# Rows of three blocks moved within SBUF in place of a store and a reload, in a Fourier mixing layer with an MLP

## The chip, the cores and the metric

One core of a Trainium2 chip runs the whole kernel. The metric is device time in microseconds. One execution is profiled as well; its trace gives the start and duration of every instruction on PE (TensorE), DVE (VectorE), ACT (ScalarE), POOL (GpSimd) and SP (SyncE, which here only issues DMAs), and of the DMA traffic.

## The reference

For one sequence of 2048 rows of 640 columns (fp32), a layer norm is followed by two branches that are summed with the input:

```python
xn = _layernorm(x, axis=-1)
return x + _A_ref(xn, seq_re, seq_im, hid_re, hid_im) + _B_ref(xn, w1, b1, w2, b2)

# A: real part of a DFT along the hidden and then the sequence dimension
a = jnp.einsum("bsd,ed->bse", x, dft_hid_re)
b = jnp.einsum("bsd,ed->bse", x, dft_hid_im)
y = jnp.einsum("ts,bse->bte", dft_seq_re, a) - jnp.einsum("ts,bse->bte", dft_seq_im, b)

# B: an MLP of 640 -> 1536 -> 640
h = _gelu(jnp.einsum("bsd,df->bsf", x, w1) + b1)
return jnp.einsum("bsf,fd->bsd", h, w2) + b2
```

The four DFT matrices are inputs: 640 x 640 (called wr and wi in the kernel) and 2048 x 2048 (cr and ci).

## The kernel before, in words

**Arithmetic.** PE multiplies in a rounded fp32 form. Each operand is split into a high half, which ACT makes (`high`), and a low half, which DVE makes as the difference (`low`); a product is then three matmuls, high by high, high by low and low by high (`product`, lines 308 to 310; in `hidden`, line 326). Many products are formed by schemes with fewer multiplications and more sums, and the sums of the operands ("forms") are made on DVE ahead of the matmuls.

**Blocks.** The rows are worked in four blocks of 512 (block 0 to 3), each as four tiles of 128 rows (`xt[c]`, c from 0 to 15). The MLP of block 0 comes first. A loop over i from 0 to 9 (the steps of `background(i)`) does for each of twelve groups of 128 MLP columns the hidden product `hidden(i + 2)` (15 matmuls), the GELU and split of the result (tile hs), and `output(i)` (15 matmuls on W2), so a step is 30 matmuls. W1 and W2 are loaded by SP, split by `prep_w1` and `prep_w2` and kept in places (`PLACES`: xab0 to xab3, xc01, xc23, as, r01, rt2), which later hold other things. In between, `background(i)` prepares blocks 1 and 2, which are called "a" and "b".

**Rows.** A block's tiles are loaded by SP (`load_x`), DVE takes the statistics (`ln_stats`, two instructions of 320 columns and a small one for each tile), `ln_scale` makes the reciprocal deviations, and `ln_apply` normalises in place. Then `put_rows` stores the tiles from POOL's queue to a DRAM tensor xs, and `load_z` loads them again from there in another arrangement, z: partition q * 32 + r of z holds quarter q of the columns of the rows r, 32 + r, 64 + r and so on. From z, DVE's 32 x 32 transposes (`transpose_z`) give what PE needs with the columns on partitions. xs is read once more, much later: `by_chunks` copies it to xn, from which the Fourier part takes its rows. Block 0 goes another way: PE transposes its normalised tiles into five PSUM banks (`transpose_x`), and ACT and DVE split these into XT. One of its tiles (`last`) is normalised on ACT, the others on DVE.

**Pairs.** `pair(k)`, k from 0 to 5, does the hidden products of blocks 1 and 2 together on two groups of columns, with seven windows of matmuls; it has six points (`beside_pair(k, at)`, in the order 2, 5, 6, 3, 7, 4) at which other work is put on the engines: the sums of block 0 (`finish(0, ...)`: a bias on ACT, a turn on DVE, an add into xo on POOL), their store to ys (`store_sums`), and the forms of wr and wi (`load_w`, `turn_w`, and `prep_w(j, n)` with n from 0 to 2 for each fifth j; they lie in the tile wst and are stored to DRAM as wits). zc is a copy of a window's result that ACT makes behind the GELU of the pair's first group.

**Between.** After the pairs, a loop over p does the output products of block 2 from units kept in DRAM (`load_unit`), and `between(p)` does beside it the sums of block 1 (xo(1), loaded by `load_xo(1, ...)` into the place xab2), the rows of block 3, the turns of these at p of 7 to 9, and the weights for block 3. `OBANKS` gives the PSUM banks of each block's five output groups; the fourth and fifth group of block 2 use the banks that the fourth and fifth of block 1 leave.

**The rest** is the hidden product of block 3 and the Fourier part: eight stages of sequence products and two of hidden products (`hidden_beside`), whose results are turned, added and stored (`store`).

**Order.** The program writes out the order of each engine's instructions by hand, and every engine runs its own in that order. An instruction that waits therefore holds all that stand behind it on its engine, and so do a DMA's waits on the queue that issues it (SP, POOL or ACT). Tiles with a tag share a place with `bufs` copies; a new tile waits until the last reader of the old one is done, a DMA that reads it included.

Of the kernel before, what the change touches and what calls it, by code (L numbers as in the profile page):

```python
# [20 lines left out]
NGATE = 4  # L21
# [5 lines left out]
def kernel(  # L27
# [134 lines left out]

    row_places = rows.tile([P, NC, D], F32, name="row")
# [5 lines left out]
    def chunked(ap):  # L169

        return ap.rearrange("p (c q i) -> p q c i", q=Q, i=B)
# [63 lines left out]
    def ln_apply_chunked(dst, c):  # L235

        m = MV[:, slot[c]]
        nc.vector.tensor_scalar(
            chunked(dst),
            xt[c].rearrange("p (q c i) -> p q c i", q=Q, i=B),  # L240
            m[:, 0:1],
            m[:, 3:4],
            op0=ALU.subtract,
            op1=ALU.mult,
        )
# [70 lines left out]
    def hidden(g):  # L316
        i = g % NF
        acc = bank((5 if g < NF else 0) + g % 3)
        kinds = ((0, 0), (0, 1), (1, 0))
        steps = [(j, k) for j in range(ND) for k in range(3)]  # L320
        if g == 0:

            steps.sort(key=lambda s: s[1] == 1)
        for n, (j, k) in enumerate(steps):
            a, b = kinds[k]
            nc.tensor.matmul(  # L326
                acc, W1[i][:, a, j * P : (j + 1) * P], XT[j][:, b], start=n == 0, stop=n == len(steps) - 1
            )
        return acc
# [321 lines left out]
    for c in (1, 0, 2, 3):  # L651
        load_x(c)
# [19 lines left out]
    for q in range(Q):  # L672
        nc.sync.dma_start(b2c[q * B : (q + 1) * B], b2[q * DQ : (q + 1) * DQ].rearrange("(c i) -> i c", i=B))

    for p in PLACES:
        open_place(*p)
# [5 lines left out]
    def transpose_x(c):  # L682
        for j in range(ND):
            nc.tensor.transpose(tacc[j][:, c * P : (c + 1) * P], xp[:, c, j * P : (j + 1) * P], ident)
# [19 lines left out]
    nc.scalar.activation(xp[:, last], xp[:, last], AF.Copy, scale=MV[:, last, 3:4])  # L704
# [8 lines left out]
    load_w1(4)  # L713
    acc0 = hidden(0)
# [7 lines left out]

    def background(i):

        if i == 0:
            for c in range(NC):
                ln_apply(c, put=False)
            A["rows_b"] = zo_tile("rows_b", (P, NC, D))
            for c in range(2 * NC, 3 * NC):
                load_x(c, home=A["rows_b"])  # L730
            for c in range(NC):
                put_rows(c)
        if i == 1:
            ln_stats(8)
            ln_stats(9)
            for c in range(NC, 2 * NC):
                load_x(c)
        if i == 2:
            ln_stats(10)
            ln_stats(11)  # L740
            ln_scale(NC)
            for c in range(2 * NC, 3 * NC):
                ln_apply(c)
            Z["b"] = zo_tile("z_b")
            load_z(Z["b"], 2)
        if i == 3:
            for c in range(NC, 2 * NC):
                ln_stats(c)
        if i == 4:
            ln_scale(NC)  # L750
            for c in range(NC, 2 * NC):
                ln_apply(c)
            Z["a"] = as_z(row_places)
            load_z(Z["a"], 1)
        if i == 5:
            new_forms(0, "vb", "ua", "va")
            make_forms("b", "vb0", "vb1", "ob0")
        if i == 6:
            new_forms(3, "t1")
            make_forms("a", "ua0", "ua1", "oa0")  # L760
        if i == 7:
            make_forms("a", "va0", "va1")
        if i >= 7:
            (ua, va), (ub, vb) = ((Z[k][:, :, : 2 * B], Z[k][:, :, 2 * B : 4 * B]) for k in "ab")
        if i == 7:
            add(ub, ub, ua, ALU.subtract)
        if i == 8:
            make_forms("b", "t10", "t11")
            add(vb, vb, ub, ALU.subtract)
        if i == 9:  # L770
# [102 lines left out]
    def finish(t, *es, home=None):  # L873

        for e in es:
            add_block(xo[t], e, oacc[t][e], f"ot{t}_{e}", bias=b2c[:, e : e + 1], **(home or {}))
# [5 lines left out]
    def store_sums(t):  # L882
        for k, (c0, c1) in enumerate(YCOLS):
            nc.gpsimd.dma_start(ys[k][t], xo[t][:, :, c0:c1])
# [5 lines left out]
    def beside_pair(k, at):  # L890

        if k == 0:
            if at == 5:
                make_forms("a", "t30", "t31")
            if at == 6:
                make_forms("a", "t40", "t41")
                load_w(0, 0)
                load_w(1, 0)
            if at == 4:
                finish(0, 0, 1)  # L900
            return
        j = k - 1
        if k == 1:
            if at == 2:
                finish(0, 2, home=in_zt)
            if at == 5:
                finish(0, 3, home=in_zt)
                finish(0, 4)
            if at == 6:
                store_sums(0)  # L910
# [6 lines left out]
        steps = {7: (0,), 4: (1,)} if k == 1 else {3: (0,), 7: (1, 2) if k == LASTK else (1,), 4: () if k == LASTK else (2,)}  # L917
        if k == 2 and at == 5:
            prep_w(0, 2)
# [7 lines left out]
        if k == 1 and at == 7:  # L927
            A["wst"] = zo_tile("wst", (P, NB * DQ), F32R)
# [69 lines left out]
    def between(p):  # L998
# [4 lines left out]
        if p == 1:  # L1003
            finish(1, 3, 4, home=in_zt)
            ln_stats(14)
        if p == 2:
            ln_stats(15)
            ln_scale(NC)
            for c in range(3 * NC, 4 * NC):
                ln_apply(c)  # L1010
# [391 lines left out]
    def hidden_beside(b, n):  # L1402
# [68 lines left out]
        v1 = lambda: add(s(1, "v1"), s(1, "v1"), x_)  # L1471
        pre = [v1] if n == 17 and not last else []
# [4 lines left out]
            3: [to(ya[:, :, : 2 * B], x_, f"ya1_{ta}")],  # L1477
            4: [t2(0)],
# [12 lines left out]
            17: [v1, yb2, yb2] if last else [yb1, yb2],  # L1491
# [144 lines left out]
```

## Time and profile before

| | |
|---|---|
| runs | 883.66, 880.26, 881.50 us; median 881.5 |
| the profiled execution | 883.43 us, of which the traced span is 881.6 |
| mean granted clock of TensorE | 0.988 |
| matmuls | 3711, of which 19 warm the clock up and 20 transpose block 0 |
| bytes | 124.92 MB read from and 51.38 MB written to HBM |

In the rows of a timeline stand the start in us, the time that the instruction (or a merged group of xN) covers, the engine, the line, the operation, the tiles (out<-in), and in brackets the idle time of the engine just before and what ended it. `POOLq`, `SPq` and `ACTq` are the queues that issue DMAs. A matmul's duration of 0.39 us is that of one in a pipeline; the distance of two starts says what it costs. Instructions of different kinds overlap a little on DVE and ACT as well.

### The profile page before, as it was taken

What the parts mean: (1) busy time and instruction counts of PE and PEld (TensorE: products, weight loads), DVE (VectorE), ACT (ScalarE), POOL (GpSimd) and SP (SyncE); (2) the same over time, 40 slices, a digit from 0 to 9 for tenths busy, and PEclk for the clock granted to TensorE, in tenths of its full rate; (3) what the DMA queues carried; (4) which work ended last, traced back from release to release, by engine and by line L of the source; (5) the groups of instructions that cost most, each with busy time, mean ns of one, the idle gap of its engine ahead of it and who ended that gap; (6) DMA issues with size and microseconds to landing.
All of it is one profiled execution on the core that took longest, in us unless ns stands there. A gap on an engine that the chain in (4) does not pass through costs nothing.

```text
span 881.6 us, 10526 instructions
## 1 busy us (share of the span) xinstructions
PE 853.3 (97%) x3711; PEld 700.4 (79%) x3711; DVE 682.6 (77%) x888; ACT 366.7 (42%) x527; POOL 79.2 (9%) x111
## 2 busy tenths in 40 slices
PE   7998998999969999999999999999999999999997
PEld 6886776888748888888888888888888888888885
DVE  6786975875734477998989888888977988886586
ACT  6554564655414456543443434332232432323241
POOL 0230043333240500000000000000000000000000
PEclk9999999999978999999999999999999999999999
DMA  7985559988988695987774259946475679904364
GB/s 195 297 264 122 112 143 280 308 236 285 256 244 202 155 355 229 168 167 173 185 161 149 59 145 324 247 96 179 115 186 183 223 214 217 337 19 173 120 166 102
DMA packets 200035, 171.76 MB, mean 195 GB/s; under 512 B 65232, under 2 KB 171216, under 8 KB 199344
## 3 DMA queue, kind: packets, MB, share of 16 engines
q1 hardware_dynamic: 187168, 142.13, 60.5%
q0 software_dynamic: 7536, 28.06, 9.3%
q10 hardware_dynamic: 5280, 0.92, 0.5%
q8 instruction: 29, 0.48, 0.2%
q14 instruction: 22, 0.18, 0.1%
HBM read 124.92 MB, written 51.38 MB: 200 GB/s over the span
## 4 chain that ended last, share of the span: by engine, by line
PE 80%; DMA 8%; DVE 5%; SPq 2%; issue 2%; POOL 1%; ACT 1%; DVEq 0%; ACTq 0%; POOLq 0%
PE banks L309 25%; PE banks L310 25%; PE banks L308 25%; PE banks L326 5%; DMA w1r<-in_B_w_dram 3%; DMA xs<-row 2%; DMA row<-in_A_x_dram 1%; DVE xab L186 1%; SPq L286 1%; SPq L399 1%; DMA row<-xs 1%; DMA rows_b<-in_A_x_dram 1%; PE banks L666 1%; DVE st L212 1%; DVE w1f L186 0%
## 5 line engine op out<-in xcount | busy, mean ns | idle before, releaser
L308 PE MATMUL banks<-as,xab 128*128 128x512 f32 x407 | 158.3, 389 | 0.0
L310 PE MATMUL banks<-as,xab 128*128 128x512 f32 x407 | 158.3, 389 | 0.0
L309 PE MATMUL banks<-as,xab 128*128 128x512 f32 x407 | 158.3, 389 | 0.0
L183 ACT ACTIVATE as<-r 128x1024 fp32r<-128x1024 f32 x80 | 85.0, 1062 | 173.6 <-PE banks L310 148.7
L186 DVE TENSOR_TENSOR as<-r,as 128x1024 fp32r<-128x1024 f32 x80 | 97.2, 1216 | 38.8 <-ACT as L183 38.8
L309 PEld LDWEIGHTS banks<-as,xab 128*128 128x128 f32 x407 | 76.4, 188 | 16.0
L308 PEld LDWEIGHTS banks<-as,xab 128*128 128x128 f32 x407 | 76.4, 188 | 15.9
L310 PEld LDWEIGHTS banks<-as,xab 128*128 128x128 f32 x407 | 76.4, 188 | 15.8
L308 PE MATMUL banks<-as,xc 128*128 128x512 f32 x224 | 87.1, 389 | 0.0
L309 PE MATMUL banks<-as,xc 128*128 128x512 f32 x224 | 87.1, 389 | 0.0
L310 PE MATMUL banks<-as,xc 128*128 128x512 f32 x224 | 87.1, 389 | 0.0
L183 ACT ACTIVATE as<-rt 128x1024 fp32r<-128x1024 f32 x32 | 34.0, 1062 | 69.8 <-PE banks L310 57.9
L326 PE MATMUL banks<-xt,xab 128*128 128x512 f32 x240 | 56.8, 390 | 0.2 <-ACT xt L183 0.2
L186 DVE TENSOR_TENSOR hs<-ab,hs 128x512 fp32r<-128x512 f32 x36 | 26.3, 732 | 34.2 <-ACT hs L183 33.9
L326 PEld LDWEIGHTS banks<-xt,xab 128*128 128x128 f32 x240 | 44.7, 188 | 10.2 <-ACT xt L183 1.3
L309 PEld LDWEIGHTS banks<-as,xc 128*128 128x128 f32 x224 | 42.0, 188 | 8.8
L310 PEld LDWEIGHTS banks<-as,xc 128*128 128x128 f32 x224 | 42.0, 188 | 8.7
L308 PEld LDWEIGHTS banks<-as,xc 128*128 128x128 f32 x224 | 42.0, 188 | 8.7
L308 PE MATMUL banks<-hs,xc 128*128 128x512 f32 x120 | 46.9, 391 | 1.3 <-DVE ot L385 1.3
L309 PE MATMUL banks<-hs,xc 128*128 128x512 f32 x120 | 46.8, 390 | 0.2 <-DVE hs L186 0.2
L310 PE MATMUL banks<-hs,xc 128*128 128x512 f32 x120 | 46.7, 390 | 0.0
L186 DVE TENSOR_TENSOR as<-rt,as 128x1024 fp32r<-128x1024 f32 x32 | 38.8, 1212 | 5.3 <-ACT as L183 5.3
(213 smaller groups left out, 1661.4 us busy)
## 6 DMA issues: line engine op xcount, KB each, us to landing
raw<-in_A_dft_seq_re_dram SPq DMA_DIRECT2D x64, 256.0 KB, 5.6
raw<-in_A_dft_seq_im_dram SPq DMA_DIRECT2D x64, 256.0 KB, 5.2
w1r<-in_B_w_dram SPq DMA_DIRECT2D x144, 80.0 KB, 3.4
wit<-wst POOLq DMA_DIRECT2D x15, 384.0 KB, 4.0
ws<-wit SPq DMA_DIRECT2D x15, 384.0 KB, 5.5
xn<-xs SPq DMA_DIRECT2D x4, 1280.0 KB, 7.0
wit<-wst POOLq DMA_DIRECT2D x20, 256.0 KB, 4.4
forms_ab<-xab SPq DMA_DIRECT2D x4, 1280.0 KB, 7.3
```

The lines of the kernel that those rows point to most:

```text
L183: nc.scalar.activation(h, s, AF.Copy)
L186: nc.vector.tensor_tensor(l, s, h.bitcast(F32), op=ALU.subtract)
L212: nc.vector.bn_stats(st[:, h, :], xt[c][:, h * half : (h + 1) * half])
L286: eng.dma_start(t[q * B : (q + 1) * B], v[q, :, :, f0 : f0 + P])
L308: nc.tensor.matmul(acc, wh, mh, start=first, stop=False, skip_group_check=goes_on)
L309: nc.tensor.matmul(acc, wh, ml, start=False, stop=False, skip_group_check=goes_on)
L310: nc.tensor.matmul(acc, wl, mh, start=False, stop=last, skip_group_check=goes_on)
L326: nc.tensor.matmul(acc, W1[i][:, a, j * P : (j + 1) * P], XT[j][:, b], start=n == 0, stop=n == len(steps) - 1)
L399: nc.sync.dma_start(t[q * B : (q + 1) * B], v[:, :, s0 : s0 + B])
L666: nc.tensor.matmul(wacc, warm[:, :P], warm, start=True, stop=True)
```

## The change

**Rows in SBUF.** `put_z(z, rows)` makes z straight from the normalised tiles: 16 DMAs from POOL's queue, each from 32 partitions to 32 others, with runs of 160 numbers. It takes the place of `load_z` for blocks 1, 2 and 3. `put_rows` follows it for all tiles of the block, so xs is written as before. The tiles of block 2 are loaded right after XT's split into the place r01, and those of block 1 in step 0 into the place rt2 (`rows_in`); both belong to later parts of W2, so these two places are opened for W2 in steps 4 and 7, and not at the start. The statistics, forms and sums of blocks 1 and 2 move to earlier steps; step 9 has none of them left.

**Start.** The tiles of block 0 are loaded in the order 0 to 3. They are normalised and transposed in two parts, columns 0 to 255 and 256 to 639. W1 of the first group is split by hand: its high half on ACT between the two parts, its low half on DVE behind both. `hidden(0)` and `hidden(1)` use new orders of their matmuls. `NGATE` changes which of three warm-up tiles each of the 19 warm-up matmuls reads: 7, 3 and 9 in place of 4, 4 and 11; the loads of w1 go into the same buffers. The loads of b2 come later.

**Sums and forms.** The sums of block 0 are stored as soon as each part is complete. The forms of the first fifth of wr and wi (j of 0) move from points 7, 4 of pair 1 and 5 of pair 2 to point 4 of pair 1 and points 2 and 5 of pair 2. The sums of block 1 are added on DVE in place of POOL.

**End.** The last 32 columns of each quarter of a block's result are turned the other way and added into the PSUM bank in `hidden_beside`, so that the final turn writes the result and no add follows.

```diff
-NGATE = 4
+NGATE = (7, 10)
+    def rows_in(tag):
+        return place(tag, (P, 4096), F32)[:, : NC * D].rearrange("p (k d) -> p k d", k=NC)
 # hidden(g)
-            steps.sort(key=lambda s: s[1] == 1)
+            steps = FIRST
+        if g == 1:
+            steps.sort(key=lambda s: s[1] == 2)
+    FIRST = [(0, 0), (1, 0), (0, 2), (1, 2), (2, 0), (2, 2), (0, 1), (3, 0), (3, 2)]
+    FIRST += [(1, 1), (4, 0), (4, 2), (2, 1), (3, 1), (4, 1)]
-    for c in (1, 0, 2, 3):
+    for c in range(NC):
         load_x(c)
-        warm = warms[min(k // NGATE, 2)]
+        warm = warms[sum(k >= n for n in NGATE)]
-    for p in PLACES:
+    for p in PLACES[:7]:
         open_place(*p)
-    nc.scalar.activation(xp[:, last], xp[:, last], AF.Copy, scale=MV[:, last, 3:4])
-    for c in (0, 2, last, 3):
-        if c != last:
-            ln_apply_chunked(xp[:, c], c)
-        transpose_x(c)
-    prep_w1(0)
+    W1[0], first_w1 = slots[1, 0], w1r.pop(0).rearrange("p a b -> p (a b)")
+    for j0, j1 in ((0, 2), (2, ND)):
+        part = xp[:, last, j0 * P : j1 * P]
+        nc.scalar.activation(part, part, AF.Copy, scale=MV[:, last, 3:4])
+        if j0 == 0:
+            nc.scalar.activation(W1[0][:, 0], first_w1, AF.Copy)
+        for c in (0, last, 2, 3):
+            if c != last:
+                ln_apply_chunked(xp[:, c], c, j0, j1)
+            transpose_x(c, j0, j1)
+    nc.vector.tensor_tensor(W1[0][:, 1], first_w1, W1[0][:, 0].bitcast(F32), op=ALU.subtract)
     for j in range(ND):
         split(XT[j][:, 0], XT[j][:, 1], tacc[j])
+    A["rows_b"] = rows_in("r01")
+    for c in range(2 * NC, 3 * NC):
+        load_x(c, home=A["rows_b"])
     load_w1(3)
     load_w1(4)
+    # the four loads of b2c, which stood before open_place
+    def put_z(z, rows):
+        for a in range(NC):
+            for q in range(Q):
+                nc.gpsimd.dma_start(
+                    z[q * B : (q + 1) * B].rearrange("r (c a) d -> r a c d", a=NC)[:, a],
+                    rows[a * B : (a + 1) * B, :, q * DQ : (q + 1) * DQ],
+                )
 # background(i), as it is after the change
+        if i == 0:
+            for c in range(NC):
+                ln_apply(c)
+            A["rows_a"] = rows_in("rt2")
+            for c in range(NC, 2 * NC):
+                load_x(c, home=A["rows_a"])
+            for c in range(2 * NC, 3 * NC):
+                ln_stats(c)
+        if i == 1:
+            ln_scale(NC)
+            Z["b"] = zo_tile("z_b")
+            for c in range(2 * NC, 3 * NC):
+                ln_apply(c, put=False)
+            put_z(Z["b"], A["rows_b"])
+            for c in range(2 * NC, 3 * NC):
+                put_rows(c)
+            ln_stats(NC)
+            ln_stats(NC + 1)
+        if i == 2:
+            ln_stats(NC + 2)
+            ln_stats(NC + 3)
+            ln_scale(NC)
+            Z["a"] = as_z(row_places)
+            for c in range(NC, 2 * NC):
+                ln_apply(c, put=False)
+            put_z(Z["a"], A["rows_a"])
+            for c in range(NC, 2 * NC):
+                put_rows(c)
+        if i == 4:
+            open_place(*PLACES[7])
+            new_forms(0, "vb", "ua", "va")
+            make_forms("b", "vb0", "vb1", "ob0")
+        if i == 5:
+            make_forms("a", "ua0", "ua1", "va0")
+        if i == 6:
+            new_forms(3, "t1")
+            make_forms("a", "oa0", "va1")
+            add(ub, ub, ua, ALU.subtract)
+        if i == 7:
+            open_place(*PLACES[8])
+            make_forms("b", "t10", "t11")
+            add(vb, vb, ub, ALU.subtract)
+        if i == 8:
+            turn_x("t20", "b")
+            turn_x("t21", "b")
+            add(ua, vb, ua, ALU.subtract)
+            add(va, va, vb, ALU.subtract)
+            load_xo(0)
 # beside_pair(k, at)
-            if at == 6:
-                store_sums(0)
+            # store_sums(0, 0) at point 4 of pair 0, (0, 1) and (0, 2) behind finish(0, 3) and finish(0, 4)
-        steps = {7: (0,), 4: (1,)} if k == 1 else {...}
-        if k == 2 and at == 5:
-            prep_w(0, 2)
+        steps = {4: (0,)} if k == 1 else {...}
+        if k == 2 and at in (2, 5):
+            prep_w(0, 1 if at == 2 else 2)
 # between(p)
-            finish(1, 3, 4, home=in_zt)
+            finish(1, 3, 4, home=in_zt, eng=nc.vector)
+            Z["z"] = zo_tile("z3")
             for c in range(3 * NC, 4 * NC):
-                ln_apply(c)
-            Z["z"] = zo_tile("z3")
-            load_z(Z["z"], 3)
+                ln_apply(c, put=False)
+            put_z(Z["z"], row_places)
+            for c in range(3 * NC, 4 * NC):
+                put_rows(c)
-            finish(1, p - 4)
+            finish(1, p - 4, eng=nc.vector)
 # hidden_beside and the end
+        def last_columns():
+            A["end"] = A["rt2"][:, 0, 0, 0]
+            nc.vector.transpose(A["end"].rearrange("p (n i) -> p n i", i=B), ya[:, :, 3 * B : 4 * B])
+        end = lambda: add(bank(X + 1), bank(X + 1), A["end"])
+            2: [last_columns] if last else [],
-            17: [v1, yb2, yb2] if last else [yb1, yb2],
+            17: [v1, end, yb2, yb2] if last else [yb1, yb2],
-        add_turned(d, turned(bank(X + k - 2), f"yt_{k}"))
+        if k == 3:
+            nc.vector.transpose(d, bank(X + 1).rearrange("p (n i) -> p n i", i=B))
+        else:
+            add_turned(d, turned(bank(X), f"yt_{k}"))
```

More of the change, by code (lines that the diff above doesn't have):

```diff
@@ L671 @@
     load_w2(2)
-    for q in range(Q):
-        nc.sync.dma_start(b2c[q * B : (q + 1) * B], b2[q * DQ : (q + 1) * DQ].rearrange("(c i) -> i c", i=B))
-    for p in PLACES:
+    for p in PLACES[:7]:
         open_place(*p)
@@ L680, with transpose_x @@
     xp = zo_tile("xp", (P, NC, D))
-    def transpose_x(c):
-        for j in range(ND):
+    def transpose_x(c, j0, j1):
+        for j in range(j0, j1):
             nc.tensor.transpose(tacc[j][:, c * P : (c + 1) * P], xp[:, c, j * P : (j + 1) * P], ident)
@@ L720 @@
     load_w1(5)
+    def put_z(z, rows):
+        for a in range(NC):
+            for q in range(Q):
+                nc.gpsimd.dma_start(
+                    z[q * B : (q + 1) * B].rearrange("r (c a) d -> r a c d", a=NC)[:, a],
+                    rows[a * B : (a + 1) * B, :, q * DQ : (q + 1) * DQ],
+                )
     def background(i):
@@ L729, in background @@
             for c in range(2 * NC, 3 * NC):
-                load_x(c, home=A["rows_b"])
-            for c in range(NC):
                 put_rows(c)
-        if i == 1:
-            ln_stats(8)
-            ln_stats(9)
-            for c in range(NC, 2 * NC):
[L737 to L742, printed above, removed]
-                ln_apply(c)
-            Z["b"] = zo_tile("z_b")
-            load_z(Z["b"], 2)
@@ L765, in background @@
-        if i == 7:
-            add(ub, ub, ua, ALU.subtract)
-        if i == 8:
+            make_forms("a", "oa0", "va1")
+        if i >= 6:
+            (ua, va), (ub, vb) = ((Z[k][:, :, : 2 * B], Z[k][:, :, 2 * B : 4 * B]) for k in "ab")
+        if i == 6:
+            add(ub, ub, ua, ALU.subtract)
+        if i == 7:
+            open_place(*PLACES[8])
             make_forms("b", "t10", "t11")
             add(vb, vb, ub, ALU.subtract)
-        if i == 9:
+        if i == 8:
             turn_x("t20", "b")
@@ L871, in keep, with finish, store_sums @@
         nc.gpsimd.dma_start(gs[g % NF], a)
-    def finish(t, *es, home=None):
+    def finish(t, *es, home=None, eng=nc.gpsimd):
         for e in es:
-            add_block(xo[t], e, oacc[t][e], f"ot{t}_{e}", bias=b2c[:, e : e + 1], **(home or {}))
+            add_block(xo[t], e, oacc[t][e], f"ot{t}_{e}", eng, bias=b2c[:, e : e + 1], **(home or {}))
     def by_chunks(t):
         nc.sync.dma_start(xn[:, t * B : (t + 1) * B], xs[t * TB : (t + 1) * TB].rearrange("(n r) d -> n r d", r=B))
-    def store_sums(t):
-        for k, (c0, c1) in enumerate(YCOLS):
+    def store_sums(t, *ks):
+        for k in ks or range(len(YCOLS)):
+            c0, c1 = YCOLS[k]
             nc.gpsimd.dma_start(ys[k][t], xo[t][:, :, c0:c1])
@@ L900, in beside_pair @@
                 finish(0, 0, 1)
+                store_sums(0, 0)
             return
@@ L907, in beside_pair @@
                 finish(0, 3, home=in_zt)
+                store_sums(0, 1)
                 finish(0, 4)
-            if at == 6:
-                store_sums(0)
+                store_sums(0, 2)
         if at == 6:
@@ L915, in beside_pair @@
             turn_w(1, j)
-        steps = {7: (0,), 4: (1,)} if k == 1 else {3: (0,), 7: (1, 2) if k == LASTK else (1,), 4: () if k == LASTK else (2,)}
-        if k == 2 and at == 5:
-            prep_w(0, 2)
+        steps = {4: (0,)} if k == 1 else {3: (0,), 7: (1, 2) if k == LASTK else (1,), 4: () if k == LASTK else (2,)}
+        if k == 2 and at in (2, 5):
+            prep_w(0, 1 if at == 2 else 2)
         if at == 3:
@@ L926, in beside_pair @@
                 load_x(13)
-        if k == 1 and at == 7:
+        if k == 1 and at == 4:
             A["wst"] = zo_tile("wst", (P, NB * DQ), F32R)
```

21 lines of the change are left out of this document (4 added, 17 removed).

## The prediction

> **What bounds the kernel now.** I read the page first, then the busy time of each engine by stretch, then PE's own waits, and at each wait the timeline of the four engines and the DMA queues around it.
>
> ```profile
> span 881.6 us, 10526 instructions
> PE 853.3 (97%) x3711; PEld 700.4 (79%) x3711; DVE 682.6 (77%) x888; ACT 366.7 (42%) x527; POOL 79.2 (9%) x111
> ```
>
> PE is the bound, but 97% flatters it: a matmul that runs at the halved clock counts as busy too. The stretches show this better (columns: stretch, its length, busy time and instructions of PE, PEld, DVE, ACT, POOL, granted clock, DMA share, GB/s):
>
> ```profile
> 60.00:100.00 40.00, 35.76 (x151) 28.69 (x150) 30.28 (x46) 19.39 (x33) 2.61 (x4) 0.96 0.52 132
> 120.00:160.00 40.00, 35.63 (x147) 27.80 (x146) 27.66 (x59) 20.46 (x45) 17.58 (x23) 0.96 0.78 240
> 220.00:280.00 60.00, 50.99 (x198) 40.03 (x198) 33.83 (x57) 20.51 (x34) 15.17 (x16) 0.89 0.92 236
> 400.00:600.00 200.00, 200.00 (x884) 165.61 (x883) 173.27 (x154) 76.51 (x78) 0.00 (x0) 1.00 0.69 173
> 860.00:881.60 21.60, 15.64 (x69) 12.57 (x67) 14.98 (x17) 2.76 (x3) 0.00 (x0) 0.97 0.48 98
> ```
>
> At full clock one matmul starts every 200/884 = 0.226 us. Lost against that: 40 - 151 x 0.226 = 5.9 us in 60 to 100, 6.8 in 120 to 160, 15.3 in 220 to 280, 6.0 at the end. The first matmul on data starts at 13.9 (below). Nothing the change touches lies elsewhere. Who PE waited for (total us, times, longest):
>
> ```profile
> PE banks L309 <- DVE hs L186: 6.1, 2, 5.9
> PE banks L326 <- ACT as L183: 3.2, 1, 3.2
> ...
> PE banks L308 <- ACT hs L183: 2.4, 1, 2.4
> PE banks L308 <- ACT ab L345: 2.2, 1, 2.2
> ...
> PE banks L310 <- DVE w1f L186: 1.0, 1, 1.0
> ```
>
> The rest of those losses is slower clock after a wait. For PE alone (busy, granted clock, DMA share, GB/s):
>
> ```profile
> 138.00:148.00 10.00, 7.52 (x26) 0.83 1.10 300
> ```
>
> Here 10 - 26 x 0.226 = 4.1 us are lost, and the wait in it was 2.2.
>
> **The change part by part.** *The start.*
>
> ```profile
> 10.49 0.83 ACT L704 ACTIVATE xp<-xp,mv 128x640 f32<-128x640 f32 x1 [0.85 <-DVE mv L224]
> 10.49 1.66 DVE L238 TENSOR_SCALAR xp<-row,mv 128x640 f32<-128x640 f32 x3
> ...
> 11.23 0.73 ACT L183 ACTIVATE xab<-w1r 128x640 fp32r<-128x640 f32 x1
> ...
> 13.23 2.56 ACT L183 ACTIVATE xt<-banks 128x512 fp32r<-128x512 f32 x5 [1.27 <-PE banks L684]
> ...
> 13.88 10.64 PE L326 MATMUL banks<-xt,xab 128*128 128x512 f32 x45 [0.25 <-ACT xt L183]
> ```
>
> Today ACT's first XT form waits until 13.23 for all 20 transposes. With the columns cut 2 to 3, DVE's first part takes 2/5 of 1.66, and ACT runs 0.33 + 0.73 + 0.50 us from 10.49, so that form starts at 12.05: 1.2 us gained, ACT now the limit. The low half of w1 ends later on DVE, but the new order asks for it third, and the low halves of x late. The larger first warm-up group holds the w1 loads back by about a microsecond; the last rows of x, on which the statistics wait, then share DMA with less. That is worth 0 to 1.0, or costs up to 0.7 where w1 itself comes late. I take 0.6, 1.8 in all, between 0.5 and 2.2. The b2c loads and the rows of block 2 swap places on SP, four issues for four.
>
> *Rows of blocks 1 and 2.*
>
> ```profile
> 24.65 2.17 DVE L228 TENSOR_SCALAR row<-row,mv 128x640 f32<-128x640 f32 x4
> ...
> 40.81 2.18 DVE L228 TENSOR_SCALAR rows_b<-rows_b,mv 128x640 f32<-128x640 f32 x4
> ...
> 63.80 2.61 POOL L263 DMA_DIRECT2D row<-xs  x4 [8.46 <-DMA xs<-row]
> ...
> 68.55 3.56 PE L326 MATMUL banks<-xt,as 128*128 128x512 f32 x15
> ...
> 73.30 1.30 DVE L267 STREAM_TRANSPOSE ztua<-row 128x512 f32<-128x512 f32 x2 [7.54 <-DMA row<-xs]
> ...
> 78.72 5.02 PE L326 MATMUL banks<-xt,as 128*128 128x512 f32 x15 [3.21 <-ACT as L183]
> ```
>
> Block 1's way through memory holds DVE until 73.30, and the W1 of the hidden product at 78.72 stands behind it. In its place POOL issues 16 small copies a block for 4 reloads (0.65 each); the stores remain, but nobody waits for them. A copy inside SBUF is not in the trace. The nearest is a store, which has as many runs (durations in ns, least, median and most):
>
> ```profile
> L233 POOL DMA_DIRECT2D xs<-row x12: 539/539/870, 25.6 to 241.2; - x12
> ...
> DMA to landing us min/median/max: 3.7/5.1/8.4
> ```
>
> I take 0.60 an issue, a little over the median, so 9.6 us a block against 2.6, and 4 us to land; the ends are 0.54 and 0.87. DVE: block 2's statistics (4 x 1.1) now follow 26.8 at once, then some 3.4 us of hs, weights and a scale, then its apply: 36.8 in place of 43.0. Copies to 46.4, four stores to 48.8. Block 1 needs four statistics more, a scale, a step's hs and weights (2.3) and its apply, to 46.7; copies to 58.4, landed near 62. Three forms (turn and low half of 0.65 each, 4.0 us), then hs and W1 (1.5): 67.5, for the product at 68.55. That is one microsecond of slack and no stall: the 3.2 us of waiting and its 1.2 of cold clock come back. DVE gets about 2 us more than a step of 6.8 holds in each of steps 0 to 2; hs and weights that are wanted 1 to 10 us later cover it, and I charge 0.4. Take 4.0, from 3 to 4.4. The last two sums, moved from step 9 to 8, free DVE for w1f: 1.2 more (the 1.0 wait and its restart), 0.8 at least.
>
> *The forms of wr and wi.*
>
> ```profile
> 130.11 3.43 POOL L884 DMA_DIRECT2D ys<-xo  x3
> ...
> 139.97 1.12 ACT L183 ACTIVATE wst<-row 128x256 fp32r<-128x256 f32 x4 [7.10 <-DMA gs<-ab]
> ...
> 141.72 0.50 PE L308 MATMUL banks<-xab,w1f 128*128 128x512 f32 x1 [2.23 <-ACT ab L345]
> ...
> 148.22 0.58 ACT L183 ACTIVATE zc<-banks 128x512 f32<-128x512 f32 x1
> ```
>
> The stores of those sums took this long to land:
>
> ```profile
> DMA to landing us min/median/max: 4.9/6.8/7.7
> ```
>
> The profile names gs, but the place that wst takes is that of the sums being stored: the third issue, near 132.3, plus 7.7 gives 140. Behind it on ACT stood the GELU for which PE waited. The stores now go out one by one as the sums are done, the last 1 to 2 us earlier, and wst comes after that GELU. But the second group of forms now stands ahead of the next GELU. Today these forms take ACT and DVE in turns from 139.97 to the end of zc at 148.8; in the new order as long, about 9, from 137.5 to 146.5. PE wants zc 24 matmuls after 139.5, at 144.9. A stall of 1.6 with 1.4 of slow clock (2.2 brought 1.9 above) replaces 4.1: gain 1.1, between -1 and 3.4. The Trainium skill, TensorE: Matmul & The Clock Gate, Part 1, has the clock halve after about one idle window of 3.4 us; by it the shorter stall stays warm and the gain would be 2.5. The row disagrees (2.2 us idle, clock 0.83), and I keep the row.
>
> *Block 1's last sums, and block 3's rows.*
>
> ```profile
> 220.05 5.68 SPq L378 DMA_DIRECT2D xab<-in_A_x_dram  x4
> ...
> 223.83 0.71 DVE L385 STREAM_TRANSPOSE ot<-banks 128x512 f32<-128x512 f32 x1
> ...
> 226.67 0.49 PE L308 MATMUL banks<-hs,xc 128*128 128x512 f32 x1 [0.34 <-DVE ot L385]
> ...
> 236.24 3.38 POOL L387 TENSOR_TENSOR xab<-xab,ot 128x512 f32<-128x512 f32 x2 [16.60 <-DMA xab<-in_A_x_dram]
> ...
> 246.45 0.55 SPq L880 DMA_DIRECT2D xn<-xs  x1
> ...
> 250.94 0.72 DVE L385 STREAM_TRANSPOSE ot<-banks 128x512 f32<-128x512 f32 x1 [10.03 <-POOL xab L387]
> ```
>
> Today POOL's adds stand behind the reload, DVE waits 10.03 for a buffer, PE 5.9 and then 2.4. With the adds on DVE that goes. But the first add needs xo(1), which lands at 236.2: POOL could wait 16.6 us there, DVE cannot. Behind the add stand the turn that frees PE's bank (the 226.67 row), two statistics, the scale and the applies. Add and turn end near 237.6, so PE starts 11.0 later; today two stalls cost 15.3 less 5.9 and 2.4, some 6 us, in slow clock, so 3.0 for this one: 14.0. Second add 0.7, statistics 2.2, hs 0.7, scale 1.1, apply 2.2: 244.5. Copies to 254.1, stores to 256.5, landed near 261, and only then does SP pass the store to xn (246.45 today); w1 behind it comes near 267 and holds back an hs by about 1.6 (0 to 5). 14.0 + 1.6 = 15.6 against 15.3: -0.3, between -4 and 2. Block 3's copies themselves, wanted near 255, land by 258, with hs two groups ahead of PE as cover. The adds (0.7 each) hide beside groups of 3.4 us.
>
> *The end.*
>
> ```profile
> 875.68 0.72 DVE L1191 STREAM_TRANSPOSE yt<-banks 128x512 f32<-128x512 f32 x1 [1.73 <-PE banks L310]
> 876.43 0.69 DVE L464 TENSOR_TENSOR yo<-yo,yt 128x512 f32<-128x512 f32 x1
> ```
>
> The last add goes: 0.7. Its two replacements on DVE lie beside matmuls, but push three stores 0.7 later, against the last one: 0.5, from 0.2 to 0.7.
>
> The sum: 1.8 + 4.0 + 1.2 + 1.1 - 0.3 + 0.5 = 8.3 us. The profiled execution took 883.4, 1.9 over the median of 881.5; 883.4 - 8.3 = 875.1, on the median 873.2. I say 873.5.
>
> **The rivals.** *DVE isn't held at 226* (xo(1) comes in time, or the turn isn't behind the add): then 14.0 goes as well, about 860. For it: DVE has little work there. Against: the loads go into a place that the pair's last window reads, so they cannot start earlier, and DMA is 0.92 busy.
>
> *The forms pile up*: w1 behind xn costs the full 5 and the pair gains nothing: 873.5 + 3.4 + 1.1 + 1, about 879.
>
> *The stall at 78 only changes its cause*, the longer steps of DVE holding W1 as block 1 did: 4.0 lost again, 878. For it: 1 us of slack. Against: copies are the only thing there that can be late by much.
>
> *The copies are dear, and it gets slower.* If each of the 36 issues from 36.8 on costs 0.87, the longest store, block 1 lands at 72.1 and the product at 68.55 waits until 77.6: 9 and 2 of slow clock in place of the 4.4 now. Block 3's copies come 4.3 later, 5 more behind xn. 873.5 + 4.0 + 6.6 + 5 = 889. It decides from about 0.75 us an issue. For it: DVE is busy all the time beside them. Against: the median store, issued beside the same DVE work, takes 0.54. The Trainium skill, SBUF — State Buffer, on the shared ports (the trap that DVE blocks a POOL-issued DMA), warns that such an issue of 620 ns becomes about 3100 beside a DVE pass in a two-port mode; by it block 1 alone would come some 90 us late. The longest row here, 870 ns, gives it little.
>
> **How the numbers follow.** Forecast 0.52; DVE not held 0.12; pile-up 0.18; cause changed 0.08; dear copies 0.10. Own range of the forecast 868 to 878. From 862 to 882 leaves out the dear copies and part of the second case. A measurement tells about 0.5% from no change, 4.4 us: faster is below 877.1. That holds nearly all of the first two cases and a little of the next two, 0.69; same takes the rest of the third and the fourth, 0.21; slower is the dear copies, 0.10.
>
> **What would show it.** The first XT matmul near 12; no PE wait between 60 and 100, and copies of 0.6 each; PE waiting for zc in the third pair; DVE's add in xo(1) waiting some 11 us and PE's longest wait on the turn before it; xn stored near 261; no add after the last turn. The forecast is wrong if xo(1) lands early, or if the mean of the copies passes 0.75.

## The result, and the profile after

The changed kernel takes 887.9 us (median of 6 runs, 886.09 to 889.22) against 881.0 for the kernel before in the same comparison: a ratio of 1.0073, with a 95% interval of 1.0052 to 1.0094. It is slower by 0.7%, where 873.5 was forecast, and lies outside the range of 862 to 882. The profiled execution of it took 887.41, of which the span is 885.6; that of the kernel before has a span of 881.6. So the two traces differ by 4.0 us, of the 6.8 between the medians: the profiled execution of the kernel before lies 2.4 over its median, that of the changed kernel 0.5 under. The terms below are those of the traces.

The page's first lines, the busy time by stretch (columns as in the prediction), and PE's waits, all of the changed kernel:

```profile
span 885.6 us, 10569 instructions
PE 852.0 (96%) x3711; PEld 700.2 (79%) x3711; DVE 686.2 (77%) x897; ACT 367.3 (41%) x528; POOL 90.1 (10%) x142
```

```profile
60.00:100.00 40.00, 35.42 (x144) 28.61 (x143) 28.12 (x42) 18.66 (x31) 4.96 (x10) 0.91 0.56 144
...
220.00:280.00 60.00, 44.83 (x178) 35.76 (x177) 33.76 (x62) 20.48 (x32) 14.32 (x23) 0.86 0.82 216
400.00:600.00 200.00, 200.00 (x884) 165.59 (x883) 173.08 (x154) 76.14 (x78) 0.00 (x0) 1.00 0.67 170
```

```profile
PE banks L312 <- DVE ot L395: 12.9, 2, 11.2
PE banks L332 <- ACT as L187: 4.6, 1, 4.6
PE banks L312 <- ACT hs L187: 3.5, 1, 3.5
PE banks L312 <- ACT zc L187: 3.2, 2, 2.4
```

Most of the loss lies in two stretches. In 60 to 100, PE gets 144 matmuls done where it got 151, and in 220 to 280, 178 in place of 198; the start and the pairs gain a part of it back. Where no edit reaches, 400 to 600, nothing changed.

A busy share doesn't give a sum. A better ledger is the start of the same group of matmuls in both traces, because PE does the same work between two of them. First the kernel before, then the changed one (PE's timeline: start, time covered, engine, line, operation, tiles):

```profile
24.35 0.39 PE L308 MATMUL banks<-hs,xc 128*128 128x512 f32 x1
...
90.38 0.39 PE L308 MATMUL banks<-hs,rt 128*128 128x512 f32 x1
...
103.95 0.39 PE L308 MATMUL banks<-hs,rt 128*128 128x512 f32 x1
...
223.45 0.39 PE L308 MATMUL banks<-hs,xc 128*128 128x512 f32 x1
...
276.35 2.88 PE L326 MATMUL banks<-xt,xab 128*128 128x512 f32 x12
```

```profile
22.17 0.39 PE L312 MATMUL banks<-hs,xc 128*128 128x512 f32 x1
...
92.53 0.39 PE L312 MATMUL banks<-hs,rt 128*128 128x512 f32 x1
...
104.77 0.39 PE L312 MATMUL banks<-hs,rt 128*128 128x512 f32 x1
...
223.03 0.39 PE L312 MATMUL banks<-hs,xc 128*128 128x512 f32 x1
...
280.58 2.66 PE L332 MATMUL banks<-xt,xab 128*128 128x512 f32 x11
```

| term of the forecast's sum | forecast gain | from the starts |
|---|---|---|
| start | 1.8 | 24.35 - 22.17 = 2.2 |
| rows of blocks 1 and 2 | 4.0 | 66.03 - 70.36 = -4.3 |
| w1f near 95 | 1.2 | 13.57 - 12.24 = 1.3 |
| pairs, forms of wr and wi | 1.1 | 119.50 - 118.26 = 1.2 |
| block 1's sums, block 3's rows | -0.3 | 52.90 - 57.55 = -4.7 |
| the rest, with the end | 0.5 | 605.25 - 605.02 = 0.2 |

Four of six terms are right within 0.4 us. Two are wrong, by 8.3 and 4.4, and they make nearly all of the error.

**The first of them.** POOL's queue in the changed kernel, while it issues the copies of blocks 2 and 1 (in brackets POOL's idle time and what ended it):

```profile
37.39 4.37 POOL L746 DMA_DIRECT2D z_b<-r  x8 [8.55 <-DVE r L232]
43.89 4.38 POOL L746 DMA_DIRECT2D z_b<-r  x8 [2.13 <-DMA z_b<-r]
49.69 2.17 POOL L237 DMA_DIRECT2D xs<-r  x4 [1.42 <-DMA z_b<-r]
51.85 2.20 POOL L746 DMA_DIRECT2D row<-rt  x4
54.44 0.55 POOL L746 DMA_DIRECT2D row<-rt  x1 [0.38 <-DMA xs<-r]
56.06 0.55 POOL L746 DMA_DIRECT2D row<-rt  x1 [1.07 <-DMA xs<-r]
56.91 0.55 POOL L746 DMA_DIRECT2D row<-rt  x1 [0.30 <-DMA xs<-r]
57.86 3.80 POOL L746 DMA_DIRECT2D row<-rt  x7 [0.41 <-DMA xs<-r]
62.35 1.09 POOL L746 DMA_DIRECT2D row<-rt  x2 [0.68 <-DMA row<-rt]
```

Count eight backwards from each wait: the ninth copy waits for the first, the first store (the 17th DMA) for a copy of the second eight, the fifth copy of block 1 (the 25th) for the first store. POOL goes on only when the DMA eight places earlier has landed. The trace also says why: it names the completion semaphore of each DMA, the counter that tells of its landing. POOL's DMAs take eight of them in turn (111 to 118), and the ninth copy carries a wait for number 115, which the first copy signals when it lands (43.61; the ninth starts at 43.89). So it is the program's order to wait. The copies took 5.5 us to land, more than the 8 x 0.553 = 4.4 in which eight are issued, so POOL stood still for 6.4 us in all (2.13 + 1.42 + 0.38 + 1.07 + 0.30 + 0.41 + 0.68). DVE turns block 1 at 67.22, and PE has its wait a step earlier than before, since the forms were moved up by a step:

```profile
67.22 1.30 DVE L271 STREAM_TRANSPOSE ztua<-row 128x512 f32<-128x512 f32 x2 [7.86 <-DMA xs<-rt]
```

```profile
72.64 6.44 PE L332 MATMUL banks<-xt,as 128*128 128x512 f32 x15 [4.58 <-ACT as L187]
```

Behind the wait, 15 matmuls take 6.44 us where the same 15 took 3.56 before (the 68.55 row of the prediction): 2.9 more are lost to the slow clock.

**The second.** DVE's wait for xo(1) (the row names a w1 that landed at about the same time; e4 shows the right name), PE's behind it, then POOL's copies, SP's store to xn, and ACT's wait for the w1 behind that store (w1 is what SP loads after it):

```profile
235.71 0.69 DVE L397 TENSOR_TENSOR xab<-xab,ot 128x512 f32<-128x512 f32 x1 [11.60 <-DMA w1r<-in_B_w_dram]
...
237.09 0.79 PE L312 MATMUL banks<-hs,xc 128*128 128x512 f32 x1 [11.18 <-DVE ot L395]
...
244.06 8.71 POOL L746 DMA_DIRECT2D z<-row  x16 [24.85 <-DVE row L232]
...
258.70 0.55 SPq L908 DMA_DIRECT2D xn<-xs  x1
...
270.00 0.74 ACT L187 ACTIVATE as<-w1r 128x640 fp32r<-128x640 f32 x1 [9.69 <-DMA w1r<-in_B_w_dram]
```

Here all 16 copies go out in 8.71 us without a wait. The copies of block 2 (tile z_b) and those of block 3 (tile z) differ in how long they take to land; the view of a tile has it in one line, first z_b, then z:

```profile
DMA to landing us min/median/max: 3.9/5.5/6.2
```

```profile
DMA to landing us min/median/max: 2.0/2.4/3.7
```

DMA was 1.08 busy in 36 to 50 and 0.65 in 244 to 253. The Trainium skill, DMA: Bandwidth & Descriptors, on the anatomy of a DMA issued from POOL, gives about 2.0 us plus the bytes over 436 GB/s, an estimate of 2.2 us for 80 KB; the 2.4 of block 3 agrees, the 5.5 among full queues doesn't.

### The profile page after: what moved, and what is told of

Same layout as the page of the kernel before. It is cut to its first block, busy times and chain, and to the rows that moved or that the text cites. A ratio compares the mean times of both kernels' runs of the same rounds, so it can differ in the third digit from the quotient of the medians.

```text
span 885.6 us, 10569 instructions
## 1 busy us (share of the span) xinstructions
PE 852.0 (96%) x3711; PEld 700.2 (79%) x3711; DVE 686.2 (77%) x897; ACT 367.3 (41%) x528; POOL 90.1 (10%) x142
## 4 chain that ended last, share of the span: by engine, by line
PE 77%; DMA 7%; issue 6%; DVE 5%; ACT 1%; SPq 1%; POOL 1%; DVEq 0%; ACTq 0%; POOLq 0%
PE banks L312 24%; PE banks L313 24%; PE banks L314 24%; PE banks L332 5%; DMA w1r<-in_B_w_dram 2%; DMA z_b<-r 1%; DMA xab<-in_A_x_dram 1%; SPq L290 1%; POOL z L746 1%; DMA xs<-r 1%; DMA row<-rt 1%; DMA w2r<-in_B_w_dram 1%; DVE w1f L190 1%; DVE st L216 1%; DVE row L232 0%
## 5 line engine op out<-in xcount | busy, mean ns | idle before, releaser
L312 PE MATMUL banks<-hs,xc 128*128 128x512 f32 x120 | 47.9, 399 | 12.9 <-DVE ot L395 12.9
L313 PE MATMUL banks<-hs,xc 128*128 128x512 f32 x120 | 47.7, 397 | 0.0
L314 PE MATMUL banks<-hs,xc 128*128 128x512 f32 x120 | 47.6, 397 | 0.0
```

Of the source, the lines that this page charges most:

```text
L312: nc.tensor.matmul(acc, wh, mh, start=first, stop=False, skip_group_check=goes_on)
L313: nc.tensor.matmul(acc, wh, ml, start=False, stop=False, skip_group_check=goes_on)
L314: nc.tensor.matmul(acc, wl, mh, start=False, stop=last, skip_group_check=goes_on)
```

## The experiments

All start from the changed kernel (ratio 1.0073). Ratios are to the kernel before, run on the same chip; e5 has 4 runs, e2 has 7, the others 10.

| run | median us | ratio, 95% interval |
|---|---|---|
| e1: two queues | 880.3 | 0.9990, 0.9974 to 1.0006 |
| e2: forms later | 885.0 | 1.0048, 1.0029 to 1.0066 |
| e3: adds later | 880.6 | 0.9993, 0.9977 to 1.0009 |
| e4: xn later | 881.9 | 1.0003, 0.9992 to 1.0014 |
| e5: e1, e3, e4 together | 863.1 | 0.9802, 0.9779 to 0.9826 |
| e6: half the bytes | 884.7 | 1.0043, 1.0025 to 1.0061 |
| e8: block 3 as before | 881.6 | 1.0012, 1.0000 to 1.0025 |

### e1: half of the copies of blocks 1 and 2 from SP's queue

```diff
-    def put_z(z, rows):
+    def put_z(z, rows, other=nc.gpsimd):
...
-                nc.gpsimd.dma_start(
+                (other if q % 2 else nc.gpsimd).dma_start(
...
-            put_z(Z["b"], A["rows_b"])
+            put_z(Z["b"], A["rows_b"], nc.sync)
...
-            put_z(Z["a"], A["rows_a"])
+            put_z(Z["a"], A["rows_a"], nc.sync)
```

> Of the 16 copies for each of blocks 1 and 2, the eight with odd q go out from SP's queue and not POOL's. In the changed kernel POOL issues eight copies in 4.4 us, then stops until the first has landed (5.5 us each), and block 1's copies are all in place only at 67.0, so PE waits 4.6 us at 72.6. Theory 1 (the eight transfers that one queue keeps under way are the limit, not the engines): two queues keep 16 under way, block 1 lands near 58, the stall at 72.6 goes, the kernel gains 5 to 6 us and lands near 882. Theory 2 (the 16 DMA engines are full from 34 to 67, share 1.0 to 1.1, and the bytes decide): block 1 still lands at 64 or later, the stall stays within 1.5 us of 4.6, the kernel is within 2 us of 887.9. Theory 3 (the price of an issue on POOL): refuted already by 0.553 us an issue; it would give half of the gain.

It takes 880.3 us. POOL's and SP's queues, then DVE's turn of block 1:

```profile
37.36 4.37 POOL L746 DMA_DIRECT2D z_b<-r  x8 [8.57 <-DVE r L232]
43.79 2.47 POOL L237 DMA_DIRECT2D xs<-r  x4 [2.07 <-DMA z_b<-r]
```

```profile
36.72 7.27 SPq L746 DMA_DIRECT2D z_b<-r  x8
...
48.17 8.48 SPq L746 DMA_DIRECT2D row<-rt  x8
```

```profile
61.54 1.31 DVE L271 STREAM_TRANSPOSE ztua<-row 128x512 f32<-128x512 f32 x2 [4.20 <-DMA w1r<-in_B_w_dram]
```

POOL still stops for 2.07 us after eight, now in front of a store. But SP has issued eight more copies beside it by then, and the bytes, DMA's share (1.08 in 36 to 40) and the landing (5.5 us) are as they were. So it wasn't the bytes that held the copies back: it was the ceiling of eight on one queue. Block 1 is turned at 61.54, near the 62 of the forecast, and PE has no wait from 50 to 100. The 58 that was expected here isn't reached: SP takes 8.48 us to issue its eight copies of block 1, and the last lands at 61.03. PE's first output product, and the first one on rt:

```profile
22.45 0.39 PE L312 MATMUL banks<-hs,xc 128*128 128x512 f32 x1
...
84.58 0.39 PE L312 MATMUL banks<-hs,rt 128*128 128x512 f32 x1
```

Between them lie 62.13 us, 3.9 less than before the change: that is the forecast's term of 4.0, once the ceiling is out of its way.

### e2: block 1's forms back in later steps

```diff
-        if i == 5:
-            make_forms("a", "ua0", "ua1", "va0")
         if i == 6:
             new_forms(3, "t1")
-            make_forms("a", "oa0", "va1")
+            make_forms("a", "ua0", "ua1", "oa0")
+        if i == 7:
+            make_forms("a", "va0", "va1")
...
# the three groups of sums and the turns behind them one step later too
```

> The changed kernel with block 1's forms in steps 6 and 7, t1 in step 8 and the last turns and sums in step 9, as in the kernel before; the copies stay as they are. My theory: the copies do bring block 1 sooner (67.0 against 73.3), but its forms were put a whole step of 6.8 us sooner as well, so PE meets the wait one product earlier. With the forms back in step 6, DVE reaches them near 63, waits until 67, and W1 for the next product is ready near 72.6 where PE wants it at 74.7: the 4.6 us wait and about 1.5 us of slow clock go, near 1.2 us come back at 95 where w1f is late again: 883 (881.5 to 884.5). The rival (DVE is overfull from step 0 on and would hold W1 in any case): the stall only moves to the product of step 7 or 8, within 1.5 us of 887.9.

It takes 885.0 us, between the two expectations. PE's waits from 20 to 100:

```profile
PE banks L332 <- DVE xab L190: 4.0, 3, 3.0
PE banks L314 <- DVE w1f L190: 1.9, 1, 1.9
```

The wait for as is gone, though block 1 was turned even later (71.99): so it came from the two together, late copies and forms a step sooner. In its place stands the old wait for w1f, 1.9. The wait for xab is of another kind: the last rows of block 1 landed late from HBM in this execution, and DVE waited 2.90 for them at 40.84; one trace doesn't tell whether that is usual.

### e3: the two adds into xo(1) behind p = 5's

```diff
-            finish(1, 3, 4, home=in_zt, eng=nc.vector)
+            finish(1, 3, 4, home=in_zt, eng=nc.vector, hold=True)
...
         if p == 5:
+            for f in held_adds:
+                f()
```

Here `hold` puts the add (line 397) into the list held_adds; the bias and the turn stay where they were.

> The changed kernel with the two adds into xo(1) that DVE does at p of 1 put behind the sums of p of 5; the two turns that free the banks stay. My theory: DVE's wait of 11.6 us for xo(1) is what PE waits for (11.2 us at 237). Without it the statistics of block 3, its copies and its stores come about 9.5 us sooner, and w1 behind the store to xn, for which ACT waited until 270.0, comes near 260.5; the product that waited until 271.3 starts near 262. So 9 us are gained, 879 (876 to 881), and the longest wait of PE in this stage is then that behind w1, 6 to 9 us. The rival (the hold hides other waits of the same length, DMA being full): PE waits as long for block 3's copies or for w1, and the kernel stays within 3 us of 887.9.

It takes 880.6 us. POOL's queue, then PE's longest wait from 220 to 285:

```profile
233.46 4.37 POOL L749 DMA_DIRECT2D z<-row  x8 [14.80 <-DVE row L232]
240.34 4.45 POOL L749 DMA_DIRECT2D z<-row  x8 [2.51 <-DMA z<-row]
```

```profile
PE banks L312 <- ACT hs L187: 9.2, 1, 9.2
```

The 11.2 are gone, and w1 behind xn, 3.5 in the changed kernel, now costs 9.2: PE arrives 13.5 us sooner (267.8 to 254.3, where the wait begins), the w1 only 7.8 (270.00 to 262.17). Time and waits are near what was expected. And the copies of block 3, now issued while DMA is full, meet the ceiling too: the ninth waits 2.51.

### e4: the store to xn at p = 10

```diff
-        if p == 5:
+        if p == 10:
             by_chunks(3)
```

> The changed kernel with the store of block 3's rows to xn issued at p of 10 in place of 5. My theory: SP waits at it for the stores of the rows (until 258.7), and w1 for p of 8 is issued behind it and behind its 1.3 MB, landing at 270.0 where ACT has waited 9.7 us; without it w1 lands near 255, the wait of 3.5 us at 271.3 and some 2.4 us of slow clock go: 882 (880.5 to 883.5). The rival (w1 is late because DMA is full with copies and stores, not because of the queue's order): the wait shrinks by less than 2 us and the kernel stays above 885.

It takes 881.9 us, as expected (882). DVE's add:

```profile
236.07 0.69 DVE L397 TENSOR_TENSOR xab<-xab,ot 128x512 f32<-128x512 f32 x1 [11.27 <-DMA xab<-in_A_x_dram]
```

The wait for hs is gone, so w1 stood behind xn; the only wait of PE left there is 10.9 for the turn behind this add. The add's wait stays, and here it is named rightly: xab is the place of xo(1), where the changed kernel's row had named a w1 that landed at about the same time.

### e5: e1, e3 and e4 together

> The changed kernel (887.9 us) with three of the edits tried singly put together: eight of the 16 copies of blocks 1 and 2 issued from SP's queue, the two adds into xo(1) held until p = 5, and the store to xn issued at p = 10. Theory (two separate losses, the ceiling on copies under way and DVE's wait for xo(1), the second hiding a third, w1 behind xn): all the stalls of 60 to 100 and of 223 to 276 go, 7.6 and 20.0 lost there in the changed kernel, some 860 us, with no wait of PE over 2.5 us before 280. Rival (a wait that is taken away only brings the next one to light, as the singly tried edits left 9.3 and 11.0 us behind): no more than the sum of the single gains, 7.6 + 7.3 + 6.0 = 20.9, 867 us or more, with a new wait of 4 us or more in 225 to 275.

It takes 863.1 us, 2.0% less than the kernel before (ratio 0.9802, 0.9779 to 0.9826): slower than the theory's 860, but below the rival's 867. The stretches of its trace (span 861.7) and PE's longest waits:

```profile
60.00:100.00 40.00, 40.00 (x178) 33.14 (x177) 34.41 (x52) 23.06 (x38) 0.00 (x0) 1.00 0.57 143
...
220.00:280.00 60.00, 58.27 (x252) 46.65 (x251) 39.07 (x62) 26.47 (x43) 24.98 (x31) 1.00 0.93 234
```

```profile
PE banks L312 <- ACT zc L187: 3.2, 2, 2.5
...
PE banks L312 <- DVE ot L397: 1.7, 1, 1.7
```

PE does 178 matmuls in 60 to 100 and 252 in 220 to 280, at a granted clock of 1.00; the old kernel did 151 and 198. The gain on the changed kernel, 2.7% or 24 us, is 3.4 more than the 20.5 of the single edits (from the ratios). The intervals, 1 to 2 us to either side for each ratio, are too wide for the times to prove this excess. The traces show its cause: the wait of 9.2 that e3 left and the one of 10.9 that e4 left are both gone. No wait of the rival's kind came: the longest from 220 to 280 is 1.1.

### e6: half of the bytes in each copy

```diff
-                    z[q * B : (q + 1) * B].rearrange("r (c a) d -> r a c d", a=NC)[:, a],
-                    rows[a * B : (a + 1) * B, :, q * DQ : (q + 1) * DQ],
+                    z[q * B : (q + 1) * B].rearrange("r (c a) d -> r a c d", a=NC)[:, a, :k],
+                    rows[a * B : (a + 1) * B, :k, q * DQ : (q + 1) * DQ],
...
# k = NC // 2 for blocks 1 and 2; POOL writes zeros into z_b ahead of them
```

> The changed kernel with each of the 32 copies of blocks 1 and 2 moving half of its rows (two of the four chunks; the other half of the two blocks is left out, and zeros or stale rows take its place), still 16 copies a block on POOL's queue. Theory (POOL waits when eight of its transfers are under way, and it is the bytes in flight that make each take 5.5 us): with less to move the copies land in some 4.4 us or less, POOL issues the 16 with under 0.5 us of waiting, block 1 is turned near 62 instead of 67.2, and PE's 4.6 us wait goes: about 881. Rival 1 (a landing is long whatever is moved: it is the queue itself): POOL still waits about 2 us after the eighth copy, block 1 is turned near 67, time within 1.5 of 887.9. Rival 2 (the copies' issue is the limit): the issue of one falls well below 0.553 us.

It takes 884.7 us, and neither expectation holds whole. POOL's queue:

```profile
35.71 4.25 POOL L746 DMA_DIRECT2D z_b<-r  x8 [5.23 <-DVE r L232]
42.21 4.38 POOL L746 DMA_DIRECT2D z_b<-r  x8 [2.25 <-DMA z_b<-r]
```

The median landing falls from 5.5 to 4.1 us and block 1 is turned at 63.56, with 0.9 us of PE's wait left. But POOL still goes on only 6.5 us after the first issue began, just as with twice the bytes (37.39 to 43.89), when the first copy has landed: it took 6.2 us in both kernels. For this copy at least, its own bytes aren't what makes it slow; the loads of w1 and w2 on SP's queue at that time may be, which no run shows. The issue of one stays at 0.54 us.

### e8: block 3 as before the change

```diff
-            finish(1, 3, 4, home=in_zt, eng=nc.vector)
+            finish(1, 3, 4, home=in_zt)
...
-            Z["z"] = zo_tile("z3")
             for c in range(3 * NC, 4 * NC):
-                ln_apply(c, put=False)
-            put_z(Z["z"], row_places)
-            for c in range(3 * NC, 4 * NC):
-                put_rows(c)
+                ln_apply(c)
+            Z["z"] = zo_tile("z3")
+            load_z(Z["z"], 3)
...
-            finish(1, p - 4, eng=nc.vector)
+            finish(1, p - 4)
```

> The changed kernel with block 3's part undone: its rows go through memory again (four stores, four reloads), and the adds into xo(1) are POOL's again; all else as changed. Theory (that part by itself costs what the starts of PE's groups say, 53.4 us before and 58.0 after for the same work): 4.5 faster than the changed kernel, 883.3, with the three old waits of PE back (0.3, 6 and 2.4). Rival (the older stage meets other transfers now, or the loss came from the stage ahead of it): within 2 of 887.9.

It takes 881.6 us, 0.6% or 5.4 us less than the changed kernel (from the ratios), a little more than the 4.5 expected. The two old waits are back (5.1 and 1.9), so this part of the change by itself cost what the starts say. It isn't the copies that cost it: e5 keeps them.

## Why the prediction was wrong

**The mechanisms in front of PE were right, one limit behind POOL was missing.** The step that failed is the one for block 1: "Copies to 58.4, landed near 62". The price of an issue was safe (0.60 taken, 0.553 measured, 1.7 us less over 36), and the landing too (4 taken, 4.2 for the last). What the step left out is that POOL, with eight completion semaphores in turn, doesn't issue a ninth DMA before the first has landed. Those waits are 6.4, the first copy came 0.6 later than put, so 62 + 6.4 + 0.6 - 1.7 = 67.3; measured 67.22. From there the forecast's own chain holds: 67.5 for hs and W1 became 72.64, for a product that PE wanted at 67.9. The wait of 4.6 and the 2.9 behind it, put at nothing, are most of the 8.3. The rival that the copies are dear has the right place and the wrong cause: it asked for 0.75 us an issue, and that its 889 lies near the 887.9 is luck. Neither of the two signs of being wrong that the forecast named came.

The slack of 1 us, given as a reason why nothing would be late, was less than the first wait (2.13), and by the forecast's own terms it wasn't there: it sets 67.5 against a product at its old time, 68.55, though the first term puts PE 1.8 earlier, at 66.75. Only DVE's late steps (below) moved that product back to 67.9 (68.55 - 2.2 + 1.5).

Where the argument looked in the trace of before, around these blocks, stores and reloads on POOL's queue go in fours, and no ceiling shows. SP's queue in the same trace has it: it, too, takes eight semaphores in turn, and its w1 load at 57.74 starts 0.02 us after the DMA eight places earlier has landed (57.72).

**DVE's longer steps** were charged 0.4. PE's starts from the first output product to the fifth say 1.5 (27.20 us before, 28.74 after): PE, which wants the low half of W1 there, is late in three steps running (0.3, 0.5 and 0.7).

**w1 behind xn was mis-sized.** The forecast gave it 1.6, between 0 and 5; it is 6.1, of which 3.7 is the wait and 2.4 what follows it, a second wait (0.45, for the low half of hs) and slow clock, which had not been counted. The store left sooner than forecast (258.70 for 261), but moves 1280 KB and lands only at 268.75; the four w1 loads issued right behind it, from 259.35 on, land at 269.27 to 269.89. DMA issues of the changed kernel from 252 to 272, with KB and the us to landing:

```profile
xn<-xs SPq DMA_DIRECT2D x1, 1280.0 KB, 10.0
w1r<-in_B_w_dram SPq DMA_DIRECT2D x13, 80.0 KB, 5.5
```

**Right**: DVE's add waits 11.60 and PE 11.18 (11.0 forecast), with 2.6 of slow clock (3.0, half of a "some 6" that is 7.0 by its own terms, 15.3 - 5.9 - 2.4). That this stall would be no worse than the old one held; only w1 made the stage slower. The start came as worked out, 2.2 for 1.8. PE waits for zc in the third pair, 2.4 where 1.6 was put; there the clock stayed up:

```profile
138.00:148.00 10.00, 8.13 (x36) 6.38 (x34) 6.56 (x18) 6.38 (x16) 3.00 (x5) 1.00 1.00 247
148.00:158.00 10.00, 9.51 (x41) 7.60 (x42) 8.94 (x21) 5.91 (x15) 3.30 (x7) 1.00 0.71 271
```

So a wait of 2.36 us left the clock at 1.00 here, where one of 2.23 had brought 0.83 before. The records of the granted clock tell the two apart: it changes only at the ends of stretches of 3.41 us (0.5 from 143.00 to 146.41 in the trace of before; 0.5 from 71.73 to 78.56, two of them, in that of the changed kernel). Before, PE's idle time, 139.48 to 141.72, lay nearly whole, 2.1 us, in the stretch just ahead of the slow one, 139.59 to 143.00. Here, counting on from 78.56, a stretch ends at 146.83, and cuts the idle time, 146.13 to 148.49, into 0.7 and 1.7. So where a wait falls counts beside its length; how much idle time a stretch bears, no run here measures. The Trainium skill, TensorE: Matmul & The Clock Gate, Part 1, says that the clock halves after about one idle window of 3.4 us, and that the windows run freely. This row agrees, that of before doesn't, with 2.1 us idle in one stretch. The forecast's charge of 1.4 for slow clock was too much, its wait 0.8 too short, and that the term came out (1.2 for 1.1) is luck.

The last turn is followed by no add, and w1f's wait went, as forecast.

## What to carry to other kernels

Before many small DMAs replace few large ones, count the completion semaphores that the program has for one queue, and compare the time to issue that many with the time that one takes to land: here eight, 4.4 us against 5.5. A step that is made to need its data sooner has to be weighed against the late end of that data, not its middle. And where two waits stand in a row, take both away before judging either: e3 and e4 gave 7 and 6 us alone, each with a wait of 9 us or more left, and with e1 (7) the three gave 24.

## What the runs showed of the hardware

POOL's and SP's queues had at most eight DMAs under way in every trace: the ninth on POOL's began 2.1 to 3.0 us late wherever the first needed longer than the eight issues, and at once where it didn't (block 3 of the changed kernel, landing 2.4). That is the program's limit, eight completion semaphores for POOL's DMAs and eight others for SP's, each waited for before it is used again; what the chip would hold with more of them, no run tells. In e1 SP's queue took eight copies of block 2 at the same moment beside POOL's, at a median of 0.61 us each and with their landing unchanged at 5.5; the eight of block 1 cost it 1.04 each.

A copy within SBUF of 80 KB cost POOL 0.553 us to issue while DVE was busy for 13.33 of 14 us, so no blocking of the issues by this DVE work appeared. It took 2.4 us to land at a DMA share of 0.65, 5.5 at 1.08.

After PE's wait of 11.18 us the granted clock was 0.5 for 5.3 us more (237.09 to 242.40), 2.6 us lost; after that of 4.58, 2.9 were lost. Such a restart belongs to the price of a long wait; after the wait of 2.36 none came.
